# Values and scores of a banded attention head on one tile shape, in alternating rounds

## The chip, the cores and the metric

The kernel runs on one core of a Trainium2 chip. The metric is the device time of one execution in microseconds, as the median of several runs. The engines are named as in the profile: PE is the matmul engine and PEld its weight loads, DVE is VectorE, ACT is ScalarE, POOL is GpSimd, SP issues the DMAs.

## What is computed

Eight batches of eight heads of banded attention over 576 positions, and a two-layer network over the 4608 tokens that come out. Four heads of a batch see the last 32 positions, the other four each fourth of the last 128:

```python
scores = scale * np.matmul(q, k.transpose(0, 1, 3, 2))
mask_plain = (rel >= 0) & (rel < window)
mask_dil = (rel >= 0) & (rel < window * dilation) & (rel % dilation == 0)
scores = np.where(masks[None, :, :, :], scores, -1000000000.0)
attn = np.exp(scores - np.max(scores, axis=-1, keepdims=True))
attn = attn / (np.sum(attn, axis=-1, keepdims=True) + 1e-09)
attn_out = np.matmul(attn, v)            # 64 per head
x = attn_out, heads side by side         # 4608 x 512
h = x @ w_in                             # 512 -> 2048
g = np.where(h >= 1, h, np.where(h <= -1, 0.0, (h + 1) ** 2 / 4))
out = g @ w_out                          # 2048 -> 512
```

## The kernel before

**The two layers.** Tokens go in nine tiles of 512, the 2048 inner columns in 16 chunks of 128; a step is one chunk of one tile. `layer1` makes a chunk of h in 12 products of 512 columns (L515), `layer2` adds a chunk of g to four banks of the result in 12 more (L556). Each operand is split into a high and a low part of float32r, so that three products stand for one. Between the layers a step has five operations on 128 x 512: clamp (L525, DVE), square (L531, ACT), maximum (L535, DVE), high part (L542, ACT), low part (L547, DVE).

**The attention.** Two heads make a pair; there are 32 pairs, n = 0 to 31. The first four are done in another way ("early") and are no part of this. For a later pair the 18 blocks of 32 queries of each head get their scores against 64 keys each: 36 products (L227) with 64 rows (the head's 64 dimensions), 32 weight columns and 64 columns that stream. `late_place` says where a block lies: in which group g of 32 partitions, and in which of nine columns of blocks u. Column u = 4 holds two blocks of each head. Then mask (L274, L281, or L266 for a bank pair), largest, subtract, exponential, sum, division, and 12 transposes into `pts`, over DVE, POOL and ACT.

The values (L400) are 20 products for a pair: keys in two halves of 64 rows, both heads, five groups of keys, with 64 weight columns and 96 streamed columns (64 or 32 at the ends). They add, without a first write, into a pair of banks `att` that ACT has cleared before (L154, columns 192 to 767 of 1024): the first half of the keys into the first bank, the second into the second. The results are taken out by L367 (ACT, high part) and L371 (DVE, low part).

**Row halves and banks.** The rows of a product are the partitions that its operands lie on: head j's queries and keys lie on partitions 64 j to 64 j + 63. A product of 64 rows and 32 columns uses an eighth of the array, one of 64 rows and 64 columns a quarter. Score blocks of head 0 (first row half) go to a spare bank, those of head 1 (second row half) to the second bank of `att`, and the blocks of column u = 4 of both heads to the start of the first bank of `att`.

**The order.** Up to step 15 of the first tile the order is a table of names (`FIRST`), with pairs 4 to 7 in it: their scores and values are visits of their own, and so are the scores of pair 8. From there on each pair n from 8 has a visit in PE's order, every fourth step, between `layer1` and `layer2` (`visit_step`, L588): the values of n, then the scores of n + 1, then the loads of the queries and keys of n + 2 (L119). I call these 23 visits joint; pair 31 has no successor, and its values stand alone. Pair n's clearing of `att` stands three steps ahead of its visit, behind that step's high part on ACT.

Of the kernel before, what the change touches and what calls it, by code (L numbers as in the profile page):

```python
# [6 lines left out]
F32 = mybir.dt.float32  # L7
# [21 lines left out]
EARLY = 4  # L29
# [37 lines left out]
def body(ctx, tc, qk, v_early, v, mask, mask4, w_in, w_out, out):  # L67
    nc = tc.nc
# [3 lines left out]
    pool = ctx.enter_context(tc.tile_pool(name="pool", bufs=1))  # L72
# [41 lines left out]
    def load_qk(n):  # L114
        hd = heads.setdefault(n, {})
        if "qk" not in hd:
            hd["qk"] = pool.tile([128, 1216], F32, tag="qk", name=f"qk{n}")[:, :S + KPAD]
        hd["q"], hd["k"] = hd["qk"][:, :S], hd["qk"][:, S:]
        nc.sync.dma_start(out=hd["qk"], in_=qk[n])  # L119

    def load_v(n, queue=nc.sync):
        hd = heads.setdefault(n, {})
# [27 lines left out]
    def cleared(n):  # L150

        att = ps.tile([128, 2, TOK], F32, tag="att", name=f"o{n}")
        at = flat(att)[:, 192 : 192 + S]
        nc.scalar.activation(out=at, in_=half_t.broadcast_to([128, S]), func=AF.Copy, scale=0.0)  # L154
        heads[n]["at"] = att, at

    def late_place(j, b):

        half, m, odd = b >= 10, b // 2, b % 2
        if half:  # L160
            return 3 - odd, 5 * j + m - 5
        if m < 4:
            return odd, 5 * j + m
        return (odd if j == 0 else 3 - odd), 4
# [36 lines left out]
                skip_group_check=True,  # L201
            )

    def scores(n, banks=None, at=None):
        if n < EARLY:
            return early_scores(n)
        hd = heads[n]
        cc = pool.tile([128, 704], F32, tag="c", name=f"c{n}", bufs=2)
        hd["cc"] = cc
        hd["c"] = cc[:, :576].rearrange("p (u x) -> p u x", x=KW)  # L210
        hd["st"] = cc[:, 576:603].rearrange("p (s u) -> p s u", s=3)
        if at is None:
            both, (one, two) = banks_of(banks, f"s{n}")
            hd["s"] = both, one[:, : 4 * KW], two[:, : 4 * KW], one[:, 4 * KW : 5 * KW], two[:, 4 * KW : 5 * KW]
        else:
            hd["s"] = None, *at
        todo = {}
        for j in range(2):
            for b in range(NB):
                todo.setdefault(late_place(j, b)[0] + 4 * j, []).append((j, b))  # L220
        for i in range(5):
            for tile in range(8):
                for j, b in todo[tile][i : i + 1]:
                    g, u = late_place(j, b)
                    src = hd["s"][1 + j] if u != 4 else hd["s"][3 + j]
                    r = slice(64 * j, 64 * j + 64)
                    PE.matmul(  # L227
                        out=src[QB * g : QB * g + QB, KW * (u % 5 % 4) : KW * (u % 5 % 4) + KW],
                        lhsT=hd["q"][r, QB * b : QB * b + QB],
                        rhs=hd["k"][r, QB * b : QB * b + KW],  # L230
                        start=True,
                        stop=True,
                    )

    def masks_first(n, banks=None):
# [25 lines left out]
    def masks(n, only=None):  # L261
        both, *src = heads[n]["s"]
        c, m = heads[n]["c"], msk[:, n % 4 // 2]
        rest = m[:, : 4 * KW].rearrange("p (u x) -> p u x", x=KW)
        if both is not None:
            nc.vector.tensor_tensor(  # L266
                out=by_head(heads[n]["cc"])[:, :, : 4 * KW],
                in0=both[:, :, : 4 * KW],
                in1=m[:, : 4 * KW].unsqueeze(1).broadcast_to([128, 2, 4 * KW]),
                op=ALU.add,  # L270
            )
        for j in range(2) if both is None else ():
            if only in (None, j):
                nc.vector.tensor_tensor(  # L274
                    out=c[:, 5 * j : 5 * j + 4], in0=src[j].rearrange("p (u x) -> p u x", x=KW), in1=rest, op=ALU.add
                )
        if only in (None, 2):
            apart = src[2] is not src[3]
            for j in range(1 + apart):
                r = slice(64 * j, 64 * j + 64) if apart else slice(0, 128)  # L280
                nc.vector.tensor_tensor(out=c[r, 4], in0=src[2 + j][r], in1=m[r, 4 * KW :], op=ALU.add)  # L281

    def spread(n, s):
        st = heads[n]["st"]
# [104 lines left out]
        hd["o"] = list(pieces(n, both, ops))  # L389

    def late_values(n):
        hd = heads[n]
        att, at = hd.pop("at")
        for i in range(5):
            for half in range(2):
                m = 4 * half + i
                a, z = (64, 96) if (half, i) == (1, 0) else (0, 64 if i == 4 else 96)
                r = slice(64 * half, 64 * half + 64)
                for j in range(2):
                    PE.matmul(  # L400
                        out=at[64 * j : 64 * j + 64, 64 * m + a : 64 * m + z],
                        lhsT=hd["v"][r, j, i],
                        rhs=pts[r, 5 * j + i, a:z],
                        start=False,
                        stop=True,
                        skip_group_check=True,
                    )
        hd["o"] = list(joint_pieces(n, at))
        return att

    def joint_pieces(n, at):
        b, c = divmod(n, 4)
        tok0 = b * S
        end = TOK - tok0 % TOK
        step = 1 if c < 2 else DIL
        cuts = sorted({0, min(end, S), S})
        for a, z in zip(cuts, cuts[1:]):
            t, off = divmod(tok0 + a, TOK)
            src, here = at[:, a:z], slice(off, off + z - a)
            if step == 1:  # L420
                yield src, t, c, lambda x, here=here: x[:, here]
# [164 lines left out]


    def visit_step(s, n):  # L588
        att = late_values(n)
        if n + 1 < NP:  # L590
            spare = bank(4 + s % 2, f"s{n}")
            rest = att[:, 0, :KW]
            scores(n + 1, at=[spare[:, : 4 * KW], att[:, 1, 4 * KW :], rest, rest])
        if n + 2 < NP:
            load_qk(n + 2)
        if n + 1 < NP and n % 2:
            load_v(n + 1)
# [104 lines left out]
    for n in range(8, NP):  # L702
        s = 4 * (n - 4) - 2
# [113 lines left out]
```

## Time and profile before

| | us |
|---|---|
| time, median of 3 runs | 878.5 |
| lowest and highest run | 878.21, 878.94 |
| the profiled execution | 879.35 |
| its span, first to last instruction | 877.5 |
| PE busy | 869.2 (99%) |
| DVE busy | 555.6 (63%) |
| ACT busy | 309.7 (35%) |
| granted TensorE clock, mean | 0.999 |

A busy time says how long an engine had something under way. PE works on several passes at once, and the page models their ends, so its 99% is no statement on how full the array is. A timeline merges neighbouring instructions of one group into one row, with the start of the first and the time from there to the end of the last.

### The profile page before, as it was taken

How to read it: one execution, taken by the hardware profiler on the slowest of the kernel's cores; microseconds unless marked ns; L12 is line 12 of the kernel's file. 1: busy time of each engine (PE TensorE's matmuls, PEld its weight loads, DVE VectorE, ACT ScalarE, POOL GpSimd, SP SyncE). 2: the span in 40 equal slices, each digit the busy share in tenths (PEclk: the TensorE clock that was granted, in tenths of full speed). 3: DMA queues.
4: the chain of work that ended last, by engine and by line, in shares of the span. 5: the costliest groups of instructions: out<-in, count | busy, mean ns of one | idle time of the engine just before them, and what ended most of it. 6: DMA issues, size and time to landing. Idle time of an engine off the chain costs nothing.

```text
span 877.5 us, 16764 instructions
## 1 busy us (share of the span) xinstructions
PE 869.2 (99%) x7138; PEld 712.7 (81%) x7138; DVE 555.6 (63%) x1083; ACT 309.7 (35%) x520; POOL 109.7 (13%) x81
## 2 busy tenths in 40 slices
PE   9999999999999999999999999999999999999998
PEld 7777888888888888888888888888888888888886
DVE  6898887666766676666666666667666443334332
ACT  3988633233333333323323232323332222222222
POOL 2355531110010111111111011011111000000000
PEclk9999999999999999999999999999999999999999
DMA  9981012101210021101210121102110010001001
GB/s 353 415 330 58 30 58 77 60 28 59 76 58 30 4 92 40 59 28 59 78 58 29 59 77 45 36 7 86 50 58 2 1 49 1 0 1 49 1 0 49
DMA packets 17354, 58.12 MB, mean 66 GB/s; under 512 B 1920, under 2 KB 2432, under 8 KB 15232
## 3 DMA queue, kind: packets, MB, share of 16 engines
q1 hardware_dynamic: 17280, 57.06, 18.0%
q8 instruction: 56, 0.92, 0.4%
q14 instruction: 18, 0.15, 0.1%
HBM read 47.61 MB, written 9.44 MB: 65 GB/s over the span
## 4 chain that ended last, share of the span: by engine, by line
PE 92%; ACT 4%; DVE 4%; issue 1%; ACTq 0%; DVEq 0%
PE acc L556 42%; PE h L515 42%; PE o L400 3%; PE s L227 2%; DVE pts L340 1%; PE o L227 1%; DVE m_wi L486 1%; DVE h L535 1%; DVE gl L547 1%; PE s L244 0%; ACT m_wi L473 0%; ACT y L531 0%; PE fill L138 0%; DVE y L525 0%; ACT gh L542 0%
## 5 line engine op out<-in xcount | busy, mean ns | idle before, releaser
L556 PE MATMUL acc<-wo,gh 128*128 128x512 f32 x1152 | 381.8, 392 | 0.1
L515 PE MATMUL h<-xh,wi 128*128 128x512 f32 x1152 | 357.6, 390 | 0.6 <-DVE gl L547 0.5
L556 PEld LDWEIGHTS acc<-wo,gh 128*128 128x128 f32 x1152 | 216.4, 188 | 47.0 <-ACT gh L542 0.5
L515 PEld LDWEIGHTS h<-xh,wi 128*128 128x128 f32 x1152 | 216.2, 188 | 46.3 <-DVE gl L547 1.1
L531 ACT ACTIVATE y<-y,small 128x512 f32<-128x512 f32 x144 | 104.2, 723 | 367.0 <-DVE y L525 366.9
L556 PE MATMUL acc<-wo,gl 128*128 128x512 f32 x576 | 224.8, 390 | 0.3 <-DVE gl L547 0.2
L515 PE MATMUL h<-xl,wi 128*128 128x512 f32 x576 | 224.4, 390 | 0.0
L525 DVE TENSOR_SCALAR y<-h 128x512 f32<-128x512 f32 x144 | 99.4, 690 | 148.5 <-PE h L515 147.5
L535 DVE TENSOR_TENSOR h<-h,y 128x512 f32<-128x512 f32 x144 | 100.7, 700 | 77.5 <-ACT y L531 77.2
L547 DVE TENSOR_TENSOR gl<-h,gh 128x512 fp32r<-128x512 f32 x144 | 99.4, 691 | 69.4 <-ACT gh L542 69.3
L340 DVE STREAM_TRANSPOSE pts<-c 32x256 f32<-32x256 f32 (+2 forms) x336 | 123.1, 366 | 5.7
L556 PEld LDWEIGHTS acc<-wo,gl 128*128 128x128 f32 x576 | 108.2, 188 | 22.6 <-DVE gl L547 1.0
L515 PEld LDWEIGHTS h<-xl,wi 128*128 128x128 f32 x576 | 108.2, 188 | 22.3
L542 ACT CAST gh<-h 128x512 fp32r<-128x512 f32 x144 | 84.4, 586 | 106.8 <-DVE h L535 106.1
L299 POOL TENSOR_TENSOR c<-c 128x576 f32<-128x576 f32 x28 | 32.3, 1154 | 407.7 <-DVE c L291 407.6
L321 POOL TENSOR_TENSOR c<-c 128x576 f32<-128x576 f32 x30 | 35.5, 1183 | 109.4 <-DVE c L317 109.4
L303 ACT ACTIVATE c<-c 128x576 f32<-128x576 f32 x30 | 20.6, 685 | 74.4 <-POOL c L299 64.0
L400 PEld LDWEIGHTS o<-pts,v 64*64 64x64 f32 x1120 | 24.4, 133 | 10.1 <-issue 9.9
L400 PE MATMUL o<-pts,v 64*64 64x96 f32 (+2 forms) x1120 | 28.4, 241 | 0.1
L371 DVE TENSOR_TENSOR xl<-o,xh 128x128 fp32r<-128x128 f32 (+7 forms) x68 | 26.5, 431 | 2.1 <-ACT xh L367 2.1
L367 ACT CAST xh<-o 128x64 fp32r<-128x64 f32 (+9 forms) x68 | 23.3, 398 | 2.7 <-PE o L400 2.6
L227 PE MATMUL s<-qk 64*32 64x64 f32 x1096 | 23.1, 224 | 0.5 <-issue 0.5
(100 smaller groups left out, 369.4 us busy)
## 6 DMA issues: line engine op xcount, KB each, us to landing
qk<-qk_in SPq DMA_DIRECT2D x29, 592.0 KB, 4.0
v<-v_in SPq DMA_DIRECT2D x28, 320.0 KB, 4.5
raw_wi<-w_in SPq DMA_DIRECT2D x8, 1024.0 KB, 13.0
raw_wo<-w_in SPq DMA_DIRECT2D x8, 1024.0 KB, 14.7
out<-out SPq DMA_DIRECT2D x32, 256.0 KB, 2.4
wi_first<-qk_in SPq DMA_DIRECT2D x2, 592.0 KB, 7.7
wo_first<-v_early_in SPq DMA_DIRECT2D x2, 384.0 KB, 11.1
out<-outs SPq DMA_DIRECT2D x3, 256.0 KB, 2.0
```

Of the source, the lines that this page charges most:

```text
L227: PE.matmul(out=src[QB * g : QB * g + QB, KW * (u % 5 % 4) : KW * (u % 5 % 4) + KW], lhsT=hd["q"][r, QB * b : QB * b + QB], rhs=hd["k"][r, ...
L299: nc.gpsimd.tensor_tensor(out=c, in0=c, in1=spread(n, 0), op=ALU.subtract)
L321: engine.tensor_tensor(out=c, in0=c, in1=spread(n, 2), op=ALU.mult)
L340: nc.vector.transpose(out=to, in_=c)
L400: PE.matmul(out=at[64 * j : 64 * j + 64, 64 * m + a : 64 * m + z], lhsT=hd["v"][r, j, i], rhs=pts[r, 5 * j + i, a:z], start=False, stop=Tr ...
L515: PE.matmul(out=hp, lhsT=weight("wi", f, w, slice(128 * c, 128 * c + 128)), rhs=xtile(t)[x][:, c], start=start and (c, w, x) == terms[0], ...
L525: nc.vector.tensor_scalar(out=gs[t, f][0], in0=hps[t, f], scalar1=-1.0, scalar2=1.0, op0=ALU.max, op1=ALU.min)
L531: nc.scalar.activation(out=y, in_=y, func=AF.Square, bias=half_t, scale=0.5)
L535: nc.vector.tensor_tensor(out=hp, in0=hp, in1=gs[t, f][0], op=ALU.max)
L542: nc.scalar.copy(out=g_tile("gh", t, f), in_=hps[t, f])
L547: nc.vector.tensor_tensor(out=g_tile("gl", t, f), in0=hp, in1=gh.bitcast(F32), op=ALU.subtract)
L556: PE.matmul(out=acc[m], lhsT=g[:, 128 * m : 128 * m + 128], rhs=weight("wo", f, w, slice(0, DM)), start=f == 0 and i == 0, stop=f == NF - ...
```

## The change

The value products get 32 weight columns in place of 64, twice as many of them, and so the same tile shape as the scores. In a joint visit they are no longer all ahead of the scores: `value_rounds` hands out rounds of eight, and `scores` takes one ahead of each of its own rounds of up to eight.

Since values and scores now stand in `att` at the same time, the scores there are added onto a cleared bank too, and ACT clears all 1024 columns for n above 7. And since one row half is to write one bank, the two blocks of head 1 in column u = 4 move to the first row half: copies of their queries and keys come with the load, in 160 more columns of `qk` on the first 64 partitions (L119, 1344 columns in place of 1184). `masks` then adds column 4 in one instruction of 128 rows for all visits; for the scores that stand alone these were two of 64 rows.

```diff
+        w = S + KPAD + (160 if n >= EARLY else 0)
+        hd["q"], hd["k"], hd["again"] = hd["qk"][:, :S], hd["qk"][:, S:], hd["qk"][:, S + KPAD :]
+        nc.sync.dma_start(out=hd["qk"][:, :w], in_=qk[n][:, :w])
...
-        nc.scalar.activation(out=at, in_=half_t.broadcast_to([128, S]), func=AF.Copy, scale=0.0)
+        wide = slice(0, 1024) if n > 7 else slice(192, 192 + S)
+        whole = flat(att)[:, wide]
+        nc.scalar.activation(
+            out=whole, in_=half_t.broadcast_to([128, whole.shape[1]]), func=AF.Copy, scale=0.0
+        )
...
-                todo.setdefault(late_place(j, b)[0] + 4 * j, []).append((j, b))
+                g, u = late_place(j, b)
+                todo.setdefault(g if j == 0 or u == 4 else g + 4, []).append((j, b))
         for i in range(5):
+            if rounds is not None:
+                next(rounds, None)
             for tile in range(8):
                 for j, b in todo[tile][i : i + 1]:
                     g, u = late_place(j, b)
-                    src = hd["s"][1 + j] if u != 4 else hd["s"][3 + j]
-                    r = slice(64 * j, 64 * j + 64)
+                    if j and u == 4:
+                        r, at_q, at_k = slice(0, 64), hd["again"][:, QB * (b - 8) :], hd["again"][:, QB * (b - 6) :]
+                    else:
+                        r, at_q, at_k = slice(64 * j, 64 * j + 64), hd["q"][:, QB * b :], hd["k"][:, QB * b :]
+                    src = hd["s"][1 + j] if u != 4 else hd["s"][3]
...
-                        start=True,
+                        start=at is None or not j and u != 4,
...
-            apart = src[2] is not src[3]
-            for j in range(1 + apart):
-                r = slice(64 * j, 64 * j + 64) if apart else slice(0, 128)
-                nc.vector.tensor_tensor(out=c[r, 4], in0=src[2 + j][r], in1=m[r, 4 * KW :], op=ALU.add)
+            nc.vector.tensor_tensor(out=c[:, 4], in0=src[2], in1=m[:, 4 * KW :], op=ALU.add)
...
     def late_values(n):
+        rounds = value_rounds(n)
+        for _ in rounds:
+            pass
+
+    def value_rounds(n):
...
-                for j in range(2):
+                for part in range(4):
+                    x = slice(QB * (part % 2), QB * (part % 2) + QB)
+                    j = part // 2
                     PE.matmul(
-                        out=at[64 * j : 64 * j + 64, 64 * m + a : 64 * m + z],
-                        lhsT=hd["v"][r, j, i],
+                        out=at[QB * part : QB * part + QB, 64 * m + a : 64 * m + z],
+                        lhsT=hd["v"][r, j, i, x],
...
+            yield
...
     def visit_step(s, n):
-        att = late_values(n)
+        rounds = value_rounds(n)
         if n + 1 < NP:
             spare = bank(4 + s % 2, f"s{n}")
+            att = heads[n]["at"][0]
             rest = att[:, 0, :KW]
-            scores(n + 1, at=[spare[:, : 4 * KW], att[:, 1, 4 * KW :], rest, rest])
+            scores(n + 1, at=[spare[:, : 4 * KW], att[:, 1, 4 * KW :], rest], rounds=rounds)
+        for _ in rounds:
+            pass
```

On PE a joint visit stood like this before; o is the pair of banks `att`, s the spare bank, and a row's last figures are rows and columns of the result. This is a visit of the first steps after `FIRST`, from its first value product to the first product behind it:

```order
L400 MATMUL o_1789<-pts,v_1525 64x96 [waits DMAHW5_49,PE_49,Activation_49]
L400 MATMUL o_1789<-pts,v_1525 64x32 [waits DVE_49]
L400 MATMUL o_1789<-pts,v_1525 64x96 x9
L400 MATMUL o_1789<-pts,v_1525 64x64 x4
L227 MATMUL s_1916<-qk_1728 32x64 [waits DMAHW3_49,DVE_49]
L227 MATMUL s_1916<-qk_1728 32x64 x3
L227 MATMUL o_1789<-qk_1728 32x64 x4
L227 MATMUL o_1789<-qk_1728 32x64 x8
L556 MATMUL acc_0_1749<-wo_892,gh_4_1828 128x512 [waits Activation_49]
```

All values stand ahead of the first score, and the score's wait for a load (DMAHW) and for DVE stands behind the 20th value product (repeats are left out here).

The same visit on PE in the changed kernel, from its first value product to the first product behind it:

```order
L417 MATMUL o_1884<-pts,v_1600 32x96 [waits DMAHW5_49,PE_49,Activation_49]
L417 MATMUL o_1884<-pts,v_1600 32x96 x3
L417 MATMUL o_1884<-pts,v_1600 32x32 [waits DVE_49]
L417 MATMUL o_1884<-pts,v_1600 32x32 x3
L238 MATMUL s_1991<-qk_1823 32x64 [waits DMAHW3_49,DVE_49]
L238 MATMUL s_1991<-qk_1823 32x64 x3
L238 MATMUL o_1884<-qk_1823 32x64 x4
L417 MATMUL o_1884<-pts,v_1600 32x96 x8
L238 MATMUL s_1991<-qk_1823 32x64 x4
L417 MATMUL o_1884<-pts,v_1600 32x64 x8
L238 MATMUL o_1884<-qk_1823 32x64 x4
L572 MATMUL acc_0_1844<-wo_911,gh_4_1923 128x512 [waits Activation_49]
```

Rounds of eight values and of eight scores alternate, the fifth round of scores has four; the scores' wait now stands behind eight value products, and 32 value products stand behind it (three of the pairs of rounds are left out).

## Rows read from the trace of the kernel before

**Rows 1.** The page, busy time of PE, and the chain that ended last by engine

```profile
PE 869.2 (99%) x7138; PEld 712.7 (81%) x7138; DVE 555.6 (63%) x1083; ACT 309.7 (35%) x520; POOL 109.7 (13%) x81
PE 92%; ACT 4%; DVE 4%; issue 1%; ACTq 0%; DVEq 0%
```

**Rows 2.** Waits of PE: for whom, us in total, times, longest

```profile
PE h L515 <- DVE gl L547: 0.5, 1, 0.5
```

**Rows 3.** Groups of PE by shape: passes, busy us, mean ns, idle before

```profile
L400 PE MATMUL o<-pts,v 64*64 64x96 f32 x784 | 24.7, 249 | 0.0
L227 PE MATMUL s<-qk 64*32 64x64 f32 x1096 | 23.1, 224 | 0.5 <-issue 0.5
L227 PE MATMUL o<-qk 64*32 64x64 f32 x920 | 21.7, 224 | 0.0
L400 PE MATMUL o<-pts,v 64*64 64x64 f32 x224 | 9.4, 219 | 0.1
L400 PE MATMUL o<-pts,v 64*64 64x32 f32 x112 | 8.6, 230 | 0.0
```

**Rows 4.** Timeline of one joint visit: start us, us, engine, line [idle before]

```profile
565.91 0.99 PE L400 MATMUL o<-pts,v 64*64 64x96 f32 x40
566.02 0.69 DVE L525 TENSOR_SCALAR y<-h 128x512 f32<-128x512 f32 x1 [1.74 <-PE h L515]
...
566.83 0.26 PE L227 MATMUL s<-qk 64*32 64x64 f32 x4
...
566.91 0.23 PE L227 MATMUL s<-qk 64*32 64x64 f32 x4
...
566.97 0.23 PE L227 MATMUL s<-qk 64*32 64x64 f32 x4
...
567.02 0.24 PE L227 MATMUL s<-qk 64*32 64x64 f32 x4
...
567.10 0.34 PE L227 MATMUL s<-qk 64*32 64x64 f32 x5
...
567.24 0.22 PE L227 MATMUL s<-qk 64*32 64x64 f32 x1
...
567.41 0.22 PE L227 MATMUL s<-qk 64*32 64x64 f32 x1
567.41 0.39 PE L227 MATMUL o<-qk 64*32 64x64 f32 x12
...
567.73 0.50 PE L556 MATMUL acc<-wo,gh 128*128 128x512 f32 x1
```

**Rows 5.** The two lines by themselves: ns least/median/most; the wait heading the scores

```profile
L400 PE MATMUL o<-pts,v x1120: 215/243/294, 54.4 to 685.7; 64*64 64x96 f32 x132, 64*64 64x64 f32 x37, 64*64 64x32 f32 x18
L227 PE MATMUL s<-qk x1096: 212/217/242, 33.4 to 662.6; 64*32 64x64 f32 x183
...
L227 PEldq EVENT_SEMAPHORE  x1: 51/51/51, 566.3 to 566.3; - x1
```

**Rows 6.** Groups of ACT from 137 to 690: the squares and the clearing

```profile
L531 ACT ACTIVATE y<-y,small 128x512 f32<-128x512 f32 x93 | 67.2, 723 | 244.2 <-DVE y L525 244.2
...
L154 ACT ACTIVATE o<-small 128x576 f32<-128x576 f32 x23 | 15.2, 660 | 0.0
```

**Rows 7.** Timelines of PE at two visits that hold values alone

```profile
78.97 0.50 PE L515 MATMUL h<-xh,wi 128*128 128x512 f32 x1 [0.46 <-DVE gl L547]
...
684.95 0.99 PE L400 MATMUL o<-pts,v 64*64 64x96 f32 x40
685.87 0.50 PE L556 MATMUL acc<-wo,gh 128*128 128x512 f32 x1
```

**Rows 8.** The two-part masks on DVE by shape; the page's DMA issues

```profile
L281 DVE TENSOR_TENSOR c<-s,small 64x64 f32<-64x64 f32 x10 | 2.2, 217 | 0.1
...
qk<-qk_in SPq DMA_DIRECT2D x29, 592.0 KB, 4.0
```

More of the change, by code (lines that the diff above doesn't have):

```diff
@@ L116, in load_qk @@
         if "qk" not in hd:
-            hd["qk"] = pool.tile([128, 1216], F32, tag="qk", name=f"qk{n}")[:, :S + KPAD]
-        hd["q"], hd["k"] = hd["qk"][:, :S], hd["qk"][:, S:]
-        nc.sync.dma_start(out=hd["qk"], in_=qk[n])
+            hd["qk"] = pool.tile([128, 1344], F32, tag="qk", name=f"qk{n}")
+        w = S + KPAD + (160 if n >= EARLY else 0)
+        hd["q"], hd["k"], hd["again"] = hd["qk"][:, :S], hd["qk"][:, S:], hd["qk"][:, S + KPAD :]
+        nc.sync.dma_start(out=hd["qk"][:, :w], in_=qk[n][:, :w])
     def load_v(n, queue=nc.sync):
@@ L202, in early_scores, with scores @@
             )
-    def scores(n, banks=None, at=None):
+    def scores(n, banks=None, at=None, rounds=None):
         if n < EARLY:
@@ L213, in scores @@
             both, (one, two) = banks_of(banks, f"s{n}")
-            hd["s"] = both, one[:, : 4 * KW], two[:, : 4 * KW], one[:, 4 * KW : 5 * KW], two[:, 4 * KW : 5 * KW]
+            hd["s"] = both, one[:, : 4 * KW], two[:, : 4 * KW], one[:, 4 * KW : 5 * KW]
         else:
@@ L224, in scores @@
                     g, u = late_place(j, b)
-                    src = hd["s"][1 + j] if u != 4 else hd["s"][3 + j]
-                    r = slice(64 * j, 64 * j + 64)
+                    if j and u == 4:
[3 more added lines that the diff above has]
+                    src = hd["s"][1 + j] if u != 4 else hd["s"][3]
                     PE.matmul(
                         out=src[QB * g : QB * g + QB, KW * (u % 5 % 4) : KW * (u % 5 % 4) + KW],
-                        lhsT=hd["q"][r, QB * b : QB * b + QB],
-                        rhs=hd["k"][r, QB * b : QB * b + KW],
-                        start=True,
+                        lhsT=at_q[r, :QB],
+                        rhs=at_k[r, :KW],
+                        start=at is None or not j and u != 4,
                         stop=True,
+                        skip_group_check=True,
                     )
@@ L391, in late_values @@
     def late_values(n):
+        rounds = value_rounds(n)
+        for _ in rounds:
+            pass
+    def value_rounds(n):
         hd = heads[n]
-        att, at = hd.pop("at")
+        hd["att"], at = hd.pop("at")
+        hd["o"] = list(joint_pieces(n, at))
         for i in range(5):
@@ L407, in late_values @@
                     )
-        hd["o"] = list(joint_pieces(n, at))
-        return att
+            yield
     def joint_pieces(n, at):
@@ L796 @@
     w2 = np.ascontiguousarray(moe_w_out.view(np.int64).reshape(NF, 128, DM).transpose(1, 0, 2))
+    again = np.concatenate([paired(qa)[:, 64:, 256:320], paired(ka)[:, 64:, 256:352]], axis=2)
+    again = np.concatenate([again, np.zeros_like(again)], axis=1)
     arrays = {
-        "qk_in": np.concatenate([paired(qa), paired(ka)], axis=2),
+        "qk_in": np.concatenate([paired(qa), paired(ka), again], axis=2),
         "v_early_in": v_early,
```

## The prediction

> **What bounds the kernel now.** I read the shares of the engines first, then the chain that ended last, then the waits of the matmul engine, and last a single visit, instruction by instruction. PE is busy for 99% of the span, and 92% of the chain lies on it [rows 1]. Its longest wait for another engine on the 512-column products is one of 0.5 us [rows 2]. So the time is the sum of what stands in PE's queue, and an edit is worth what it does to the stretch of PE that it touches. The edit touches two groups: the late value products (L400) and the score blocks (L227). Both are fp32, and the trace has two passes for one product: 1120 passes of L400 are 28 visits of 20 products, and the 920 passes of L227 into o are 23 joint visits of 40 [rows 3]. The other 32 passes of a joint visit's 36 score products go to s.
>
> A joint visit, taken apart [rows 4]. The values start at 565.91, the scores at 566.83, the first 512-column product behind them at 567.73: 1.82 us from the first value to that. A pass of 64 columns lasts 0.217, so the values' last pass starts at 565.91 + 0.99 - 0.217 = 566.68 and the scores' last at 567.41 + 0.39 - 0.217 = 567.58 [rows 4, 5]. The stretch is thus 0.77 (values), 0.15 (change from 64x64 to 64x32 tiles), 0.75 (scores), 0.15 (change back to the full array).
>
> What sets those 0.77 and 0.75? Inside the score burst one tile starts a pass each 0.055 us (566.91, 566.97, 567.02). In the values, a tile of the first row half runs eight passes of 96 columns and two of 64; with 0.05 until the first weights are in (294 against 243 ns), 0.77 = 0.05 + 8 x 0.082 + 0.055, so a 96-column pass holds its tile 0.082 us. The values are bound by their tiles. The scores are not: ten passes of 0.055 would be 0.55. The rows say why. Eight groups of four passes start between 566.83 and 567.10, which is 16 products; then the 17th starts at 567.10, as the first one ends, and from there on passes start singly (21 between 567.24 and 567.41, 8 ns apiece, so 16 to 17 ns a product). So **PE holds 16 products at a time, taken in order, and the 17th enters about 0.24 us after the first pass of the first one started** (567.10 - 566.83, less 0.025 that this pass waited for its weights, 242 against 217 ns) [rows 4, 5].
>
> **The change part by part.**
>
> *Joint visits (23).* Forty value products with 32 weight columns replace 20 with 64, and values and scores now run in one tile shape, in rounds of eight. Columns and passes of a tile stay as they were: each 64x32 tile streams what its 64x64 tile streamed. A tile of the first row half has 0.66 + 0.11 of values and ten score passes of 0.055. The 16 products that PE holds are now exactly one round of values and one of scores. A tile's work in such a pair of rounds is 2 x 0.082 + 2 x 0.055 = 0.27 us. But the next pair cannot start before the oldest product is out: first pass, 0.082 to its second pass, 0.24 until its place is free, 0.025 for the next weights, 0.35 in all. So a pair costs 0.35 and not 0.27: four pairs 1.40, ahead of them 0.025, and the last 12 products (eight of 64 columns, four blocks of scores) at 16.7 ns apiece 0.20, and 0.15 to the full array: 1.77 against 1.82. **The 0.15 of the tile change is won, and two thirds of it is paid back** by the places in the queue. With the ends as rows give them, 0.05 us a visit: 23 x 0.05 = 1.15 us less.
>
> The one unknown in this is whether a place comes free a fixed 0.24 after a pass starts, or later for a wider one: the 96-column pass is listed with 243 ns against 217 [rows 5]. Then a pair costs 0.377, the visit 1.88, and the edit loses 0.06. The wait that heads the scores decides for the fixed price, barely: the sequencer meets it after 20 products, hence after the second pass of the fourth value product has given its place up. The first two products' second passes start at 565.91 + 0.05 + 0.08 = 566.045; plus 0.24, plus the eight hand-overs of the last two products at 4 ns (16.7 for a product's two loads and two passes), gives 566.32; with 27 ns more, 566.35, and the wait itself comes behind that. It is listed at 566.3 [rows 5], so below 566.35. I take the fixed price.
>
> *Waits in a joint visit.* The first score product waits for DVE's bank and its qk load. It stood behind 20 value products, now behind eight of 40, some 0.7 us earlier, and 32 value products stand behind it. It is met: VectorE had been idle for 1.74 us before its first work of this step [rows 4], and the load left a visit earlier, 23.8 us (five visits from 565.91 to 684.95), with a landing of 4.0 [rows 4, 7, 8]. Price nothing. The values' readers (the casts of L367) come after the step's own g_high on ACT and wait for no end of the values, which now comes some 0.6 us later.
>
> *Lone values (28 - 23 = 5 visits).* Here the tiles hold 0.77 as before, and the queue binds: two and a half batches of 16 products, 0.025 + 2 x 0.35 + 8 x 0.0167 = 0.86, so 0.09 more (0.15 with the wider price). The last one (684.95) lies bare on PE: +0.1. The one at 77.52 is followed by PE's 0.46 us wait for VectorE [rows 7], which swallows it; the three others stand among waits for transposes: 0 to 0.1 each, I take 0.1 in all.
>
> *Lone scores (5).* Two blocks per visit move to the first row half: tiles 0 to 3 hold five products each and tiles 4 to 7 four, before two tiles of either half had five. The longest tile is still five: nothing. VectorE adds one 128-row mask where it added two of 64 rows, 217 ns less, five times [rows 8]. It can cut a wait of PE such as that of rows 2, or nothing: 0 to -0.4, I take -0.1.
>
> *ACT, SP.* The clearing of the bank pair grows from 576 to 1024 columns, 24 times: at most twice 660 ns, and ACT idles 244 us before its 93 squares, 2.6 us a step [rows 6]. Hidden; without that cover 0.5 us a visit would be late at the square. The qk load grows from 592 to 672 KB; with the bytes its landing goes from 4.0 to 4.5 [rows 8], a visit ahead of need. In the first 60 us, where the weights stream, it may push a transfer by some tenths: 0 to 0.3, I take 0.1.
>
> Sum: -1.15 + 0.1 + 0.1 - 0.1 + 0.1 = -0.95 us. The profiled execution took 879.35 (span 877.5), 0.85 above the median of 878.5, which I hold for its own scatter: **877.5 us**.
>
> **The rivals.** *B, the wide price:* places come free 0.027 later for 96 columns. 23 x 0.06 + 0.15 + 0.3 = +1.8: 880.3. For it: the listed 243 against 217. Against: the wait at 566.3. It decides as soon as a place needs over 0.26 us after a 96-column pass starts. *C, no limit by places:* the queue moves on while passes are under way, as it would if the pause at 567.10 belonged to the lone score burst (a refill, not a limit). Then the first row half's tiles set the visit: 0.025 + 8 x 0.082 + 11 x 0.055 + 0.15 = 1.43, 0.39 less, 23 times: 869.6. Against: the pause and the lone passes after it in [rows 4]. *D, a fixed price per pass:* if the 0.77 us of the values were 40 passes of 19 ns, 80 passes would take 1.55, the scores 0.75, the exit 0.15: 2.45, +0.63 a visit and +0.8 for each lone one: 894. Against: 72 score passes in 0.75 are 10.5 ns apiece [rows 4]. The Trainium skill, page "TensorEngine Tiling (Array Packing)", section Instruction Overhead, names such a price, some 60 cycles a matmul, and warns of tiling a dimension that is already small; at 2.4 GHz that would be an estimated 25 ns for each of 152 passes, 3.8 us a visit. The row of the scores speaks against it.
>
> **How the numbers follow.** My case 0.66, B 0.2, C 0.1, D 0.04. A run of this kernel can tell about 0.2%, 1.76 us, from no change. My case lies within it unless a pair of rounds is another 0.01 us shorter; I give 0.17 to that, and all of C: faster 0.27. Slower: D and a third of B, 0.1. Within: 0.63. My case's own range is 876.3 to 878.7; the range that should hold it 8 times in 10 takes in B and some of the way towards C, 875.3 to 880.4.
>
> **What would show it.** Right: in a joint visit's timeline no 0.15 gap between values and scores, one between the first value and the first 512-column product of 1.75 to 1.79 us, and four pauses of some 0.08 us in which no first pass starts, 0.35 apart; the lone values at 685 some 0.1 longer. B: pauses 0.377 apart, 1.88. C: no pauses, passes every 8 ns throughout. D: values' passes 19 ns apart. It would be wrong outright if PE waited for VectorE or a qk load inside a visit, or if the start of the 512-column products behind a visit moved from 0.15.

## The result, and the profile after

The changed kernel takes **888.32 us** (887.8 to 888.68, four runs) against 878.5: the ratio is 1.0111, 95% interval 1.0095 to 1.0127. It is 9.8 us slower; the prediction said 877.5, with a range of 875.3 to 880.4. The profiled executions have spans of 886.8 and 877.5, and the 9.3 us between them are what has to be found. In this kernel the values are L417, the scores L238, `layer1` is L531 and `layer2` L572.

The page of after: PE's share, the chain by engine, and PE's instruction packets (queue: packets, MB, share of 16 engines).

```profile
PE 871.8 (98%) x8258; PEld 714.8 (81%) x8258; DVE 553.8 (62%) x1078; ACT 318.6 (36%) x520; POOL 109.7 (12%) x81
PE 92%; ACT 2%; DVE 2%; DMA 2%; issue 1%; SPq 0%; ACTq 0%; DVEq 0%
q8 instruction: 65, 1.06, 0.5%
```

The answers to [rows 1] look harmless: PE 98%, and 92% of the chain. The third line stands on every page, and I had passed over it. On the page of before it reads

```profile
q8 instruction: 56, 0.92, 0.4%
```

PE's program grew from 7138 passes with as many weight loads to 8258: some 2240 instructions more, and nine more packets. A packet is 16 KB (1.06 MB / 65), and 8258 x 2 / 65 = 254 instructions and a few waits: **one packet carries 256 instructions of PE**, and it comes by DMA while the kernel runs.

Waits of PE, as [rows 2] (for whom: us in total, times, longest):

```profile
PE acc L572 <- ACT xh L376: 1.9, 1, 1.9
PE o L238 <- issue: 1.9, 1, 1.9
PE acc L572 <- issue: 1.1, 1, 1.1
```

Three new stops in the joint visits; the kernel before had none there, and its 512-column products never waited longer than 0.5 us [rows 2]. Two are put down to "issue", which is time in which the engine waited for nothing that the profile shows. The third is named after a cast on ACT, but that cast reads the values of this very visit; it follows them and doesn't release PE.

**A visit without a stop.** The timeline at pair 18, as [rows 4]:

```profile
383.39 0.37 PE L417 MATMUL o<-pts,v 64*32 64x96 f32 x16
...
384.13 0.38 PE L417 MATMUL o<-pts,v 64*32 64x96 f32 x8
...
384.49 0.38 PE L417 MATMUL o<-pts,v 64*32 64x96 f32 x8
...
384.85 0.36 PE L417 MATMUL o<-pts,v 64*32 64x64 f32 x7
...
385.06 0.27 PE L238 MATMUL o<-qk 64*32 64x64 f32 x4
385.26 0.50 PE L572 MATMUL acc<-wo,gh 128*128 128x512 f32 x1
```

Values and scores run into each other; the 0.15 us between them in [rows 4] is gone. The rounds of values start 0.36 to 0.37 apart, though, and it is 385.26 - 383.39 = 1.87 us from the first value to the first 512-column product: before it was 1.82, the prediction had 1.77, its rival B 1.88. In ns, from the start of the first pass to that of the last, all visits without a stop have 1727 to 1730 where before had 1675 to 1679. The products behind a visit start a little wider, too, and the distance between two visits grew from 23.81 to 23.90: 23 x 0.09 = 2.1 us.

**A visit with a stop.** The end of pair 14's:

```profile
282.42 0.36 PE L417 MATMUL o<-pts,v 64*32 64x64 f32 x7
282.56 0.24 PE L238 MATMUL o<-qk 64*32 64x64 f32 x1
282.57 0.27 PE L417 MATMUL o<-pts,v 64*32 64x64 f32 x4
284.74 0.31 PE L238 MATMUL o<-qk 64*32 64x64 f32 x7 [1.91 <-issue]
284.99 0.50 PE L572 MATMUL acc<-wo,gh 128*128 128x512 f32 x1
```

In the middle of the last round of scores nothing starts for 2.1 us. These blocks add onto the same bank and read the same load as the ones that ran just before, so neither explains the wait. The DMA view of 281 to 285 shows all that was on the queues (the first line is 40 slices of 0.1 us, busy share in tenths):

```profile
DMA  0000000000080000000000000000000000000000
...
DMA packets 1, 0.02 MB, mean 4 GB/s; under 512 B 0, under 2 KB 0, under 8 KB 0
...
q8 instruction: 1, 0.02, 2.1%
```

One packet, of PE's instructions. It starts at 282.16 and takes 1.36 us, and PE goes on at 284.74, 2.6 us after its start.

**Where the stops lie.** I counted PE's instructions (passes, weight loads and waits) in the order of the trace. Work goes on after a stop at instruction 6593 (284.74), 7105 (310.84) and 7617 (339.20), and after a fourth, shorter one in lone scores at 1729 (59.42). These are 25, 27, 29 and 6 times 256, plus 193 each time: **all four lie at the start of a block of 256.** A joint visit now has 76 products x 2 passes x 2 = 304 instructions and two waits; before it had 56 x 4 = 224 and two. So a visit can now hold a whole block. The distance between visits is 498 instructions, 14 short of two blocks, so the start of a block moves 14 places back in each visit: it stands 21 places behind the visit's first weight load for pair 13, then 35, 49 and 63 for pairs 14, 15 and 16, then 77. The three with a stop are the middle ones.

Why these: the event of the scores' two-semaphore wait, which stands 32 instructions into the visit, is listed at 281.0, as the visit's first product starts, and just so in every visit:

```profile
L417 PEldq EVENT_SEMAPHORE  x1: 51/51/51, 276.8 to 276.8; - x1
L238 PEldq EVENT_SEMAPHORE  x1: 51/51/51, 281.0 to 281.0; - x1
```

The wait at the visit's head was met 4 us earlier, at 276.8. So PE's sequencer (PEldq in these rows) runs ahead by the 32 value instructions and no further; what holds it there no run shows. A block that begins 21 places into the visit is thus entered before the visit starts, and the packet after it leaves at 254.75, 2.3 us before pair 13's visit. One that begins 35 places in is entered only when the visit runs; the packet leaves at 282.16, and the visit has used up the 256 instructions by 282.6. With 77, the next block starts 27 instructions behind the visit, among 512-column products that need 0.227 us for two instructions, and the packet is there in time.

Pair 16's stop has a second cause. Its visit starts at 334.31, and its packet leaves at 336.81, 2.5 us later where it was 1.2 for pairs 14 and 15. Until then the DMA engines were busy with loads and results (DMA view of 335 to 340, slices of 0.125 us; the 4 in the 15th is the packet):

```profile
DMA  9999989996211040009299334496889699884520
```
```profile
339.20 0.39 PE L572 MATMUL acc<-wo,gl 128*128 128x512 f32 x1 [1.12 <-issue]
```

So the stop of 1.3 us stands for the place in the block and the busy DMA engines together.

**The half clock.** The second stop has a sequel. Timeline and windows (us, busy time and count of PE, PEld, DVE, ACT, POOL, granted clock, DMA share, GB/s):

```profile
310.84 0.39 PE L572 MATMUL acc<-wo,gh 128*128 128x512 f32 x1 [1.92 <-ACT xh L376]
...
312.29 1.05 PE L572 MATMUL acc<-wo,gh 128*128 128x512 f32 x2
313.14 0.63 PE L572 MATMUL acc<-wo,gl 128*128 128x512 f32 x1
```
```profile
281.00:286.00 5.00, 3.09 (x157) 2.70 (x157) 2.56 (x5) 2.01 (x4) 0.00 (x0) 1.00 0.02 3
...
311.00:315.00 4.00, 4.00 (x12) 3.08 (x12) 1.67 (x5) 0.68 (x1) 1.15 (x1) 0.58 0.75 296
```

Two products in 0.85 us (312.29 to 313.14): seven products are 427 ns apart in place of 227, at the lower of the two clocks (512 columns in 427 ns are 1.2 GHz), 1.4 us more. The stop of the same length at 282.6 had no such sequel: the granted clock stays at 1.00.

| where the 9.3 us of span went | us |
|---|---|
| up to pair 8's visit (137.56 for 137.36), stop in lone scores within | 0.2 |
| three stops: 2.1, 2.0, 1.3 | 5.4 |
| seven products at half clock | 1.4 |
| 23 visits, 1.729 us for 1.677 | 1.2 |
| 23 stretches between visits, 22.171 us for 22.131 | 0.9 |
| pair 31's values alone, 0.93 for 0.77 | 0.2 |

### The profile page after: what moved, and what is told of

Same layout as the page of the kernel before. It is cut to its first block, busy times and chain, and to the rows that moved or that the text cites. A ratio compares the mean times of both kernels' runs of the same rounds, so it can differ in the third digit from the quotient of the medians.

```text
span 886.8 us, 18999 instructions
## 1 busy us (share of the span) xinstructions
PE 871.8 (98%) x8258; PEld 714.8 (81%) x8258; DVE 553.8 (62%) x1078; ACT 318.6 (36%) x520; POOL 109.7 (12%) x81
## 3 DMA queue, kind: packets, MB, share of 16 engines
q8 instruction: 65, 1.06, 0.5%
## 4 chain that ended last, share of the span: by engine, by line
PE 92%; ACT 2%; DVE 2%; DMA 2%; issue 1%; SPq 0%; ACTq 0%; DVEq 0%
PE acc L572 43%; PE h L531 42%; PE o L417 4%; DMA raw_wo<-w_in 1%; PE o L238 1%; PE s L238 1%; DMA wi_first<-qk_in 1%; DVE pts L349 1%; DVE m_wi L502 1%; DVE h L551 0%; ACT m_wi L489 0%; DVE gl L563 0%; ACT y L547 0%; ACT raw_wi L496 0%; ACT wi L509 0%
## 5 line engine op out<-in xcount | busy, mean ns | idle before, releaser
L572 PE MATMUL acc<-wo,gh 128*128 128x512 f32 x1152 | 382.9, 393 | 2.0 <-ACT xh L376 1.9
L531 PE MATMUL h<-xh,wi 128*128 128x512 f32 x1152 | 357.5, 390 | 0.3 <-DVE gl L563 0.3
L572 PEld LDWEIGHTS acc<-wo,gh 128*128 128x128 f32 x1152 | 216.9, 188 | 49.5 <-issue 1.3
L531 PEld LDWEIGHTS h<-xh,wi 128*128 128x128 f32 x1152 | 216.2, 188 | 46.4 <-DVE gl L563 0.9
L572 PE MATMUL acc<-wo,gl 128*128 128x512 f32 x576 | 225.8, 392 | 1.3 <-issue 1.1
L531 PE MATMUL h<-xl,wi 128*128 128x512 f32 x576 | 224.2, 389 | 0.0
L572 PEld LDWEIGHTS acc<-wo,gl 128*128 128x128 f32 x576 | 108.4, 188 | 24.5 <-issue 1.8
L531 PEld LDWEIGHTS h<-xl,wi 128*128 128x128 f32 x576 | 108.1, 188 | 22.3
L417 PEld LDWEIGHTS o<-pts,v 64*32 64x32 f32 x2240 | 41.9, 105 | 10.1 <-issue 9.9
L417 PE MATMUL o<-pts,v 64*32 64x96 f32 (+2 forms) x2240 | 49.2, 242 | 0.1
L238 PE MATMUL s<-qk 64*32 64x64 f32 x1096 | 37.2, 221 | 1.2 <-issue 1.2
L238 PE MATMUL o<-qk 64*32 64x64 f32 x920 | 35.8, 220 | 1.9 <-issue 1.9
```

Of the source, the lines that this page charges most:

```text
L238: PE.matmul(out=src[QB * g : QB * g + QB, KW * (u % 5 % 4) : KW * (u % 5 % 4) + KW], lhsT=at_q[r, :QB], rhs=at_k[r, :KW], start=at is None ...
L417: PE.matmul(out=at[QB * part : QB * part + QB, 64 * m + a : 64 * m + z], lhsT=hd["v"][r, j, i, x], rhs=pts[r, 5 * j + i, a:z], start=False ...
L531: PE.matmul(out=hp, lhsT=weight("wi", f, w, slice(128 * c, 128 * c + 128)), rhs=xtile(t)[x][:, c], start=start and (c, w, x) == terms[0], ...
L572: PE.matmul(out=acc[m], lhsT=g[:, 128 * m : 128 * m + 128], rhs=weight("wo", f, w, slice(0, DM)), start=f == 0 and i == 0, stop=f == NF - ...
```

## The experiments

The theory: (1) the visit costs more because a place in PE's queue comes free later for a wider pass, rival B of the prediction; (2) most of the time went where PE ran out of instructions, at block starts that fall into a window of the visit. Rivals: the larger load and clearing, or something in pairs 14 to 16.

**The extras alone.** The kernel before, with the larger `qk` load and the wider clearing:

```diff
+        w = S + KPAD + (160 if n >= EARLY else 0)
...
+        nc.sync.dma_start(out=hd["qk"][:, :w], in_=qk[n][:, :w])
...
+        wide = slice(0, 1024) if n > 7 else slice(192, 192 + S)
```

> The kernel before with only what the change adds off PE: the query and key load of 672 KB in place of 592, and the clearing of 1024 columns of the bank pair in place of 576. PE's program is that of before. If the loss of 9.8 us came from the larger load (a transfer that the visits or the instruction blocks wait for) or from the longer clearing, some of it shows here: 880 to 888. If it comes from PE's own program, 878.5 within 0.4, no idle time of PE without a releaser after 60 us, and joint visits of 1.82 us from the first value product to the first 512-column product.

879.08 us, ratio 1.0007 (0.9997 to 1.0016): no difference. The clearing went from the 660 ns of [rows 6] to 1033, the load to 672 KB and 4.4 us for the 4.0 of [rows 8]:

```profile
L157 ACT ACTIVATE o<-small 128x1024 f32<-128x1024 f32 x24 | 24.8, 1033 | 0.0
```

The visits stay at 1677 ns. The prediction was right to price these at next to nothing. This run has no stops, though, so it doesn't show what the larger load does to one.

**Values on 64x32 tiles, but all ahead of the scores.** The changed kernel without the alternation:

```diff
-            scores(n + 1, at=[spare[:, : 4 * KW], att[:, 1, 4 * KW :], rest], rounds=rounds)
+            for _ in rounds:
+                pass
+            scores(n + 1, at=[spare[:, : 4 * KW], att[:, 1, 4 * KW :], rest])
```

> The changed kernel, but a joint visit does all five rounds of values before the first round of scores, on the same 64x32 tiles. As many products, in another order. Theory 1 (PE's instructions come in blocks of 256, and a block that a visit uses up before the next one is there stops PE): the same count stands at the same places, so the stops stay at the same three visits (about 284, 310 and 338 us) and near 59, some 6 to 7 us in all. Theory 2 (the alternation of values and scores stops PE): no stops. On the regular visits: if a queue place comes free later for a wider pass, values alone pay it 0.04 us per 16 products above what their tiles need and the scores none, and the visit is 1.63 + 0.15 = 1.78 us, 0.10 shorter than with rounds, 886 in all under theory 1 and 879 under theory 2.

884.35, ratio 1.0065 (1.005 to 1.008). A visit of it:

```profile
641.79 1.15 PE L417 MATMUL o<-pts,v 64*32 64x96 f32 x80
642.74 0.26 PE L238 MATMUL s<-qk 64*32 64x64 f32 x4
...
643.31 0.39 PE L238 MATMUL o<-qk 64*32 64x64 f32 x12
```

The 40 value products alone take 0.95 us, where 20 with 64 columns took 0.77 and the change of tile shape 0.15: cutting them in two uses up what one tile shape wins. 16 of the 23 visits have 1691 or 1692 ns, 0.06 more than expected; the only visit with 1621 is pair 8's, the one whose first score product waits for a single semaphore, so I put 0.07 down to the two-semaphore wait, which is an instruction of its own. That rests on one visit; the other six have 1722 to 1809, and why is open but for pair 14's. Two stops are there too, at instructions 7105 and 7617 (2.0 and 0.5 us idle), the block starts of the changed kernel, and seven products at half clock. The third, at 6593, was expected and has shrunk to 0.12 us (pair 14's 1809). So alternating the rounds isn't what brings the stops; that they sit at the same instruction numbers says that the count does, and the next run moves that count.

**The same program, 128 instructions later.** 32 small products more at the start of the program:

```diff
-tab0 qk0 small52 fill2.5 fill1.5 pm0 S0 max0 max0.1 sub0 pm1 tab1 qk1 S1 max1.0 sub0.1 exp0 max1.2
+tab0 qk0 small84 fill2.5 fill1.5 pm0 S0 max0 max0.1 sub0 pm1 tab1 qk1 S1 max1.0 sub0.1 exp0 max1.2
```

> The changed kernel with 32 more of the small products that fill PE's first microseconds (84 in place of 52): 128 more PE instructions ahead of everything, half a block of 256, at about 1 us of PE in a stretch where it waits for loads anyway. Theory 1 (blocks of 256 instructions): the trace of the changed kernel has every stop at place 193 of 256 in PE's order; a visit starts 14 places earlier in a block than the one before it, and half a block is nine visits. So no stop at the visits near 281, 307 and 334 us; two or three stops of 1 to 2 us at the visits of pairs 23 to 25, 496 to 546 us. Total 886 to 890. If the stops belong to those visits' data, loads or neighbours, they stay near 281 to 339.

892.54, ratio 1.0156 (1.0141 to 1.0171). The visits of pairs 14 to 16 run through in 1728 ns. Pairs 23 and 24 stop instead, at 11201 and 11713, block starts both (43 and 45 times 256, plus 193):

```profile
527.64 0.25 PE L238 MATMUL o<-qk 64*32 64x64 f32 x3
530.66 0.21 PE L238 MATMUL o<-qk 64*32 64x64 f32 x1 [2.76 <-issue]
```

So pairs 14 to 16 have nothing of their own. The second stop is the longer one: its visit starts at 525.97, and the packet leaves at 528.40, 2.4 us later, when the loads have let go of the DMA engines (DMA view of 526 to 531, the 4 is the packet); pair 23's left 1.1 us after its visit's start.

```profile
DMA  9999989998999993100400000000000000000000
```

The total lies above the 886 to 890 expected: one stop is longer than the 1 to 2 us allowed, and the start of the program lost 4.2 us (pair 8's visit at 141.80 for 137.56). The 32 products themselves make 1.1 us of that. PE also waits for issue there, for 0.6 us at 8.2 and 2.1 us at 14.7, both at block starts (449 and 705) while the weights stream, and the granted clock is 0.78 from 10 to 20.

**Narrower values.** Every value product cut to 64 streamed columns (what a product gave to its last 32 queries is left out):

```diff
-                a, z = (64, 96) if (half, i) == (1, 0) else (0, 64 if i == 4 else 96)
+                a, z = (64, 96) if (half, i) == (1, 0) else (0, 64)
```

> The changed kernel with all value products cut to 64 streamed columns (those of 96 leave 32 columns of the values out). As many instructions, so the stops should stay where they are. It prices a queue place: with 64 columns both views say that 16 products cost 0.055 + 0.24 + 0.027 = 0.323 us. If a place comes free later for 96 columns (0.377 for a pair of rounds), the visit falls from 1.73 to 1.51 us between first and last pass, 23 x 0.216 = 5.0 us, total 883.3. If it is a fixed 0.24 (0.350), by half of that, to 1.62, total 885.8. If the tiles set the 1.73, four rounds of 96 columns lose two times 0.027 each: again 1.51, but then the timeline shows no pauses between the rounds in either kernel.

883.06, ratio 1.005 (1.0033 to 1.0067); the visits have 1510 ns, 218 less:

```profile
640.36 0.32 PE L417 MATMUL o<-pts,v 64*32 64x64 f32 x16
...
641.82 0.27 PE L238 MATMUL o<-qk 64*32 64x64 f32 x4
642.02 0.50 PE L572 MATMUL acc<-wo,gh 128*128 128x512 f32 x1
```

With the fixed price, four pairs of rounds would win 27 ns each by the shorter way to the second pass, 108 in all. They win twice that, so a place comes free 27 ns earlier as well: the wide price. The text on record has a third reading, tiles as the limit, with the same 1.51 but no pauses. The changed kernel has a pause of 83 ns behind the 33rd pass of a visit (383.69), in which no tile starts a pass, and this one has 55 ns there, so tiles alone don't set the visit. The stops stayed at the same instructions (6593, 7105, 7617).

**Every visit at the same place of its block.** An alignment ahead of the `layer1` chunk of each visit, filled with empty instructions, so that the visit starts halfway into a block; and once more with an offset of 89 in place of 8, which puts a block start 45 places into the visit:

```diff
+                if s % 4 == 0 and s < 4 * (NP - 4):
+                    PE.addr_align(256, 8)
                 layer1(*steps[s])
```

> The changed kernel with empty instructions ahead of each fourth step, so many that every joint visit begins 128 places into a block of 256 PE instructions (some 14 a visit, handled by PE's sequencer microseconds ahead of the array). No other difference. Theory 1 (a block that a visit uses up before the next one has come): no stop at any joint visit and no half-clock stretch; what is left is 0.09 us for each of 23 visits, 0.2 for the lone values and 0.9 for the stop of lone scores near 59: 881.6 (880.8 to 882.5). If the stops had another cause, they stay, and it is 888.

> As e4_align, but every joint visit begins 209 places into a block, so that the next boundary comes 47 instructions into the visit and the one after it 303 in, just before its end. In the changed kernel the visits with the boundary at 36, 50 and 64 stopped for 2.15, 2.0 and 1.3 us, and one of them ran on at half clock for 1.4. Theory 1: a stop of some 2 us in every joint visit, 23 x 2.0 = 46 us, and up to 23 x 1.4 = 32 for the clock: 925 to 965. If it is not the place in a block: as e4_align.

The first: 906.19, ratio 1.031 (1.0293 to 1.0327); the second: 975.83, from a single run. Waits of PE in the first, then in the second, then the second's span and granted clock:

```profile
PE small L146 <- issue: 15.5, 1, 15.5
PE h L531 <- issue: 7.1, 1, 7.1
PE sc L200 <- issue: 3.2, 1, 3.2
```
```profile
PE o L238 <- issue: 43.9, 22, 3.0
```
```profile
core 0: 974.0 us, clock 0.958
```

In the second, 22 of the 23 visits stop, each at a block start, 1.5 to 3.0 us each, and 18 of the stops are followed by products at half clock. The three of 2.8 and 3.0 us are the ones whose packet left 2.5 us after the visit's start, with the DMA engines over 80% busy. The whole lies 11 us above the 925 to 965 expected; waits for issue outside the visits (2.6, 2.4 and 7.2 us) alone make 12. In the first, not one of the 23 stops. But its time is far from the 881.6 that I expected, and for another reason: the program begins with 199 empty instructions ahead of the first product (15 us) and has 152 ahead of the first aligned chunk (7.1 us, and a dozen products at half clock). I had priced an empty instruction at nothing; each takes some 0.07 us (15 us / 199). The time of this kernel therefore proves nothing; its visits do, beside those of the second.

**Another order of the rounds.** Aligned in the same way; the joint visit has one round of scores, three of values, four of scores, two of values, and values that stand alone go back to 64x64 tiles:

```diff
-            if rounds is not None:
-                next(rounds, None)
+            if rounds is not None and i == 1:
+                for _ in range(3):
+                    next(rounds)
...
+                if s % 4 == 0 and s < 4 * (NP - 4):
+                    PE.addr_align(256, 8)
```

> A version made from what the runs showed: visits aligned as in e4_align, lone values on 64x64 tiles as before, and in joint visits one round of scores, three of values, the four other rounds of scores, two of values, on one tile shape. With 16 products in flight, a place free 0.24 us after a 64-column pass starts and 0.27 after one of 96, worked through product by product, this order takes 1.59 us from the first pass to the last, against 1.68 in the kernel before and 1.73 with alternating rounds. 23 x 0.08 = 1.9 us less than before: 876.6 (876.0 to 877.6). If order does not matter once the tile shape is one, it is e2's regular visit, 1.69: 878.8.

907.95, ratio 1.0334 (1.0311 to 1.0358), where 876.6 was expected, again by the empty instructions (199 and 216; waits of 15.5 and 11.7 us). The visits came out as worked out, 1589 ns, and 23.72 us apart: 0.09 less than in the kernel before. (Scores are L239 here, values L432, `layer2` L587.)

```profile
641.40 0.26 PE L239 MATMUL s<-qk 64*32 64x64 f32 x4
...
641.54 0.74 PE L432 MATMUL o<-pts,v 64*32 64x96 f32 x44
...
642.69 0.51 PE L432 MATMUL o<-pts,v 64*32 64x96 f32 x30
643.14 0.50 PE L587 MATMUL acc<-wo,gh 128*128 128x512 f32 x1
```

**The changed kernel with 512 instructions a pair, and nothing empty.** Seven 512-column products a pair are split into two of 256 columns, 14 instructions more, so that the visits no longer drift along the blocks:

```diff
+        for at, (c, w, x) in enumerate(terms):
+            halves_of = (slice(0, 256), slice(256, 512)) if 1 <= at <= parted else (slice(0, 512),)
+            for cols in halves_of:
...
+                joint = 18 <= s < 4 * (NP - 4) - 2 + 4
+                layer1(*steps[s], parted=7 if joint and s % 4 == 0 else 0)
```

> The changed kernel; seven of the twelve 512-column products of the layer1 chunk ahead of each joint visit are each split into two of 256 columns, so that a pair's stretch of PE's program has 512 instructions in place of 498 and every joint visit lies at the same place against the blocks of 256 (193 places ahead of the next block's start, where the changed kernel ran without a stop). No empty instructions. Theory of the instruction blocks: no stop at the visits of pairs 14 to 16 and no half-clock products there (6.8 us less), regular visits 1729 ns as before, each split worth 8 to 13 ns (23 x 7 of them, 1.3 to 2.1 us): 888.3 - 6.8 + 1.7 = 883.2 us, 882.5 to 884. Rival (the stops belong to those pairs for another reason, a buffer or a load): stops at 282, 309 and 338 us as before: 890 us.

883.85, ratio 1.0061 (1.0047 to 1.0075): 4.5 us less than the changed kernel, with more instructions. No joint visit stops, no product runs at half clock, the visits keep their 1728 to 1729 ns. Windows at the three places, columns as above, this kernel ahead of the changed one:

```profile
280.00:290.00 10.00, 10.00 (x188) 8.20 (x188) 5.71 (x11) 3.31 (x7) 1.16 (x1) 1.00 0.21 70
306.00:316.00 10.00, 10.00 (x113) 8.40 (x95) 6.37 (x13) 4.30 (x9) 2.21 (x2) 1.00 0.44 136
```
```profile
280.00:290.00 10.00, 8.09 (x179) 6.58 (x178) 4.44 (x9) 2.69 (x5) 1.15 (x1) 1.00 0.22 72
306.00:316.00 10.00, 8.08 (x173) 6.60 (x172) 4.36 (x9) 2.60 (x5) 1.15 (x1) 0.83 0.39 138
```

PE's busy 8.1 of 10 us becomes 10, and 0.83 of clock 1.00. The visits stand 24.014 us apart, 0.114 more than in the changed kernel, so a split costs 16 ns where I had 8 to 13, if nothing else differs. From the first value of pair 8 to that of pair 31 it is 552.3 us (556.5 in the changed kernel): 4.2 less, and the splits cost 23 x 0.114 = 2.6, so the stops and the half clock were 6.8 us, as the table above has it.

**The better order without empty instructions.** The order of the last but one, lone values of pairs 5 and 6 on 64x32 to shift the visits by 160 instructions, and three or four splits a pair (the text on record names the order of the rounds loosely; it is the one above):

```diff
+        if n in (5, 6):
+            for _ in value_rounds(n):
+                pass
+            return
...
+                layer1(*steps[s], parted=(4 if s < 52 else 3) if joint and s % 4 == 0 else 0)
```

> The order of run e7 (one round of values, one of scores, three of values, four of scores on a single tile shape, lone values on 64x64) without its empty instructions: the lone values of pairs 5 and 6 on 64x32 (80 instructions more each) and three or four split products a pair move the visits along the blocks so slowly that the next block's start stays between 103 places behind a visit's first product and nine behind the one of the block after. Theory of the instruction blocks: no stops; 23 x 0.09 us less than the kernel before, 23 x 3.4 splits of 8 to 13 ns (0.6 to 1.0 us) and two lone visits (0 to 0.3 us) more: 877.1 to 877.8 us, 0.1% under the kernel before, hardly to be told from it. Without a hold of the theory (stops at some visits wherever they lie): 880 or more.

879.57, ratio 1.001 (1.0001 to 1.0019): a miss by 2 us. No visit stops, and they have 1595 ns, 82 less than before. But the visits stand 23.825 (three splits) or 23.84 (four) apart for 23.81: outside the visit a pair lost 0.1 us, twice what three splits at 16 ns explain. The rest, but for 0.01, is the wider spacing behind a visit that the changed kernel has too (0.04) and that two aligned kernels, with and without the new order, and the ones with narrower or unmixed values don't have. What makes that spacing is open. So no version that beats the kernel before came out of this.

## Why the prediction was wrong

*What bounds the kernel.* Right as far as it went: all of the 9.3 us lie on PE. But "the time is the sum of what stands in PE's queue" assumed that the queue is always fed. The page had a line on how PE's program comes, and the sum had no term for it. This is the step that failed most: 6.8 of 9.3 us.

*Joint visits.* The gap of 0.15 went away, as said. The pair of rounds was put at 0.35, with B's 0.377 as the other end, and the choice between them rested on one wait listed at 566.3 and a limit of 566.35 [rows 5]. That was the wrong choice: the rounds came 0.36 apart on average, the visit took 1.87 where B had 1.88, and narrowing the values took off twice what a fixed price allows. B's reason, the 243 ns against 217 in [rows 5], was the stronger row; a listing to a tenth of a microsecond can't decide over 0.03. The trace itself has that wait at 566.343, 0.023 behind the fixed price's 566.32 and less than 0.01 ahead of the wide one's 566.35: unrounded, the same row leant to B. The sign named for it came out in part: of four pauses of 0.08 us the first is there (83 ns), the others are 26, 26 and 46 ns; later starts are spread over the round. Instead of 1.15 us less, the visits brought 1.2 more. The Trainium skill's price of some 60 cycles a matmul (page "TensorEngine Tiling (Array Packing)", section Instruction Overhead), weighed as rival D and read as a price that adds up over the passes of all tiles, would have made an estimated 3.8 us of the 152 passes of a visit; they took 1.73, so the trace doesn't bear that reading out here.

*Instructions.* "Forty value products replace 20" was costed as columns and queue places. The same sentence means 80 more instructions a visit and a visit longer than a block of 256. In the trace 65 packets of PE's program came while the kernel ran, and PE stood still for some of them.

*Waits in a visit.* "Price nothing" was right in that neither VectorE nor a load is waited for. But the wait's new place, 32 instructions into the visit in place of 80, is also, by the listing, how far the sequencer runs ahead, and with the block's place that decides which visits stop.

*What behind a visit moves.* The prediction asked whether the start of the 512-column products moves from 0.15; it stays at 0.146. The products that follow lose 0.04 a visit, for which it had no term.

*Lone values.* The last one: 0.16 more for 0.1 predicted, 0.15 by the wide price. *Lone scores, ACT, SP:* nothing, as the run with the extras showed, but for a stop in lone scores of some 0.7 us, of which 0.2 is left at pair 8's visit.

*The range.* It ended at 880.4, B's time, and a third of B was all that stood for slower, with D. B's mechanism alone gives 883.85 less the splits' 2.6, 881.2: outside too, by the spacing behind the visits.

## What to carry to other kernels

Count the instructions of a burst, not only its columns: where small products start every 10 ns, a block of 256 instructions is gone in 1.5 us, while its successor took 1.2 us from the start of the block to the packet's start and another 2.2 to 2.8 us to its use. A block that begins well inside such a burst (35 and 49 places in, here) and ends inside it or just behind it stops the engine; one that was entered before the burst (21), or that ends 27 instructions behind it (77), did not. Stops that are put down to "issue", that come in some repetitions of a loop and not in others, at instruction numbers of equal remainder, are this; a few split products that change the loop's length move them away. And where two rows disagree on a price by less than a listing's last digit, keep both as equals.

## What the runs showed of the hardware

- PE's program arrives in packets of 16 KB, 256 instructions; all the stops of 0.5 us or more in and just behind joint visits, 22 in the one kernel built to have them, lay at starts of such blocks.
- The packet of a stopped visit leaves about 1.2 us after the sequencer passes the start of the block before it (281.0 to 282.16), takes 0.9 to 1.4 us, and is used 2.2 to 2.8 us after it left.
- After a stop of 2 us the granted clock may fall for 3 us (0.58 in 311 to 315, products 427 ns apart for 227) or not (1.00 in 281 to 286). What decides is open.
- An empty instruction holds PE's sequencer for some 0.07 us (199 in 15 us at the start), five times the 13 ns that it is listed with (first aligned kernel):

```profile
L759 PEldq NOP  x659: 13/13/13, 0.8 to 697.1; - x165
```

- A wait for two semaphores is an instruction of its own. With all values ahead on 64x32 tiles the one visit without it took 1621 ns and most others 1691; in the kernel before and in the changed one that visit is no shorter (1679 for 1675 to 1678, 1730 for 1727 to 1730), so 0.07 us is no fixed price.
- Instruction packets compete with the loads: with the DMA engines over 80% busy the packet of a stopped visit left 1.5 to 2.5 us after the visit's start, else 1.0 to 1.3 (kernel with 22 stops), and stops of 1.5 to 1.9 us became 2.1 to 3.0.
